# A state-space scan in chunks of 64 over pairs of batches, and a shorter seam before the experts

## The chip, the cores and the metric

The kernel runs on one core of a Trainium2 chip. Its time is the device time of one execution in microseconds (us). The core has the engines PE (matrix products; its weight loads are shown as PEld), DVE (vector), ACT (activation), POOL (general purpose) and SP, which here only issues DMA transfers; transfers that POOL issues go through indices. SBUF is the on-chip memory, PSUM the memory that PE writes, HBM the main memory. A `name<-a,b` in a row is the tile written and the tiles read.

## The reference

Two parts follow each other. The first is a scan over 4 batches, 8 heads and 768 places, with 32 columns of x and 16 of state per head:

```python
cum = cumsum(log(clip(a, 1e-6, 1)))          # within a chunk
L = exp(cum[i] - cum[j]) for i >= j, else 0
y = ((C @ B.T) * L) @ x + (C @ state) * exp(cum)
state = exp(cum[-1]) * state + (B * exp(cum[-1] - cum)).T @ x
```

The result does not depend on the size of the chunk but for rounding. Its rows, 3072 tokens of 256 numbers, go to the second part, which gives each token to one of 8 experts:

```python
logits = x @ w_gate;  e = argmax(logits);  gate = softmax(logits)[e]
out = gate * (relu(x @ w1[e]) @ w2[e])       # 256 -> 1024 -> 256
```

## The kernel before, in words

**Scan.** A tile is one batch and 128 places with all 8 heads; there are 24. For each, `decay` (L152) makes the lower triangle L of products of a: PE copies the tile's row of `az` to all 128 partitions (`abc`, L158, two fp32 matmuls of 512 columns, in which one row of the identity picks one of 24 rows), and DVE runs a product scan over them (L161, two of 512). `scores` (L181) is C times B for four heads at a time, 64 rows of the array each (`g`, L187), with C written four times under a mask by POOL (`masks`, `ctm`, L148), so that each head sees its own 16 rows. `weigh` (L191) multiplies g by L on DVE. `state` (L199) adds the tile's own part A (L205) to the carried state on DVE (L209 to L213); A is 128 by 256, and a mask `smask` keeps the blocks of each head. `y` (L217) adds the carried part (L223, through `ctd`, made on POOL from a second scan `dec` on DVE) and the part of the tile (L228: 8 matmuls, each on 32 columns of the array, with all 128 rows). `rows` (L236) turns the result to one token per partition and makes the 8 logits in the same matmuls (L245); ACT copies it out of PSUM.

**Routing.** Groups of 6 tiles are routed: `choose` (L253) takes the expert, and POOL counts on tile by tile (`cnt`, L272); `rank` (L279) makes each token's place by two matmuls; `place` (L292) sends each tile's 128 rows to the expert's list `x_hbm` in HBM by an indirect DMA of POOL.

**Experts.** `m_load` (L316) reads an expert's list back (448 places), `m_xT` (L336) transposes it, `m_h` (L354) and `m_y` (L369) are the two products, `m_half` (L377) the last 64 places of two experts together, and `put` (L360) scales and scatters rows to the output.

**Order.** It is written out by hand in the main loop (L428): every engine runs its own queue in the program's order. In one turn of the loop come decay and scores of tile n, the masks of tile n + 1, state and y of tile n - 1, weigh of tile n, rows of tile n - 2, and at times choose, rank and two places. All of the experts' weights (16 MB, L139) are loaded during the scan, three transfers for every three tiles. After the last tile the places of the last six tiles follow (L458), and then everything of `over` (L301, a check on overflow) and of the experts 0 and 1's lists before the first `m_h`.

Of the kernel before, what the change touches and what calls it, by code (L numbers as in the profile page):

```python
# [9 lines left out]
FP32 = mybir.dt.float32  # L10
# [20 lines left out]
NR = N + 128  # L31


@with_exitstack
def ssd_then_moe(ctx, tc, x, a, B, BT, CT, w_gate, w1, w2, out):
# [32 lines left out]

    oh_all = route.tile([128, NT, E], BF16, name="oh_all")
    cnt = route.tile([128, NT + 1, E], BF16, name="cnt")  # L70
# [4 lines left out]
    def scan_consts():  # L75
        make_identity(nc, ident)
        nc.vector.tensor_copy(turn[:, 0:128], ident)
        nc.vector.tensor_copy(turn[:, 128 + 2 * E:], ident)
        nc.vector.tensor_copy(ident4, bc(ident[:, None, :], [128, 4, 128]))
        nc.gpsimd.memset(hsel, 1.0)  # L80
        nc.gpsimd.affine_select(out=hsel, in_=hsel, pattern=[[-NS, NH]], base=0, channel_multiplier=1,
                                compare_op=ALU.is_ge, fill=0.0)
        nc.gpsimd.affine_select(out=hsel, in_=hsel, pattern=[[NS, NH]], base=NS - 1, channel_multiplier=-1,
                                compare_op=ALU.is_ge, fill=0.0)
        nc.vector.tensor_tensor(vmask, hsel[:, 0:4], hsel[:, 4:8], op=ALU.add)  # L85
        nc.vector.tensor_copy(smask, bc(hsel[:, :, None], [128, NH, D]))

    def route_consts():
        nc.gpsimd.memset(Tmat, 1.0)
# [5 lines left out]
        nc.vector.tensor_scalar(out=rev_e, in0=iota_i, scalar1=-1.0, scalar2=float(E), op0=ALU.mult, op1=ALU.add)  # L95
        nc.vector.tensor_scalar(out=base_e, in0=iota_i, scalar1=float(NR), scalar2=None, op0=ALU.mult)
        nc.gpsimd.iota(tok_i, pattern=[[128, NT]], base=0, channel_multiplier=1)
        nc.vector.memset(cnt[:, 0, :], 0.0)
# [4 lines left out]
        nc.gpsimd.tensor_copy(zrows[:, :, DM + 1].bitcast(I32), none_i)  # L103
        for e in range(E):
            nc.sync.dma_start(out=x_hbm[e * NR:e * NR + CAP, :].rearrange("(p c) w -> p c w", c=CAP // 64),
                              in_=zrows)
# [5 lines left out]
    def clip(ap):  # L112
        nc.vector.tensor_scalar(out=ap, in0=ap, scalar1=1e-6, scalar2=1.0, op0=ALU.max, op1=ALU.min)

    def load_a():
        for b in range(NB):
            nc.sync.dma_start(out=az[b * NC:(b + 1) * NC], in_=a[b].rearrange("h (c i) -> c h i", i=128))
        clip(az)
        nc.vector.memset(az[:, :, 0:1], 0.0)  # L119

    def load(g):
        b, s0 = divmod(g * CG * 128, S)
        c0 = s0 // 128
        r = gr[g]
        T = CG * 128
        r["CT"] = ld.tile([128, T], FP32, name="ct")
        nc.sync.dma_start(out=r["CT"], in_=CT[b, :, s0:s0 + T])
        r["BT"] = ld.tile([128, T], FP32, name="bt")
        nc.sync.dma_start(out=r["BT"], in_=BT[b, :, s0:s0 + T])
        r["a"] = ld.tile([128, T], FP32, name="ar")  # L130
        nc.sync.dma_start(out=r["a"], in_=bc(a[b, :, None, s0:s0 + T], [NH, NS, T]))
        r["B"] = ld.tile([128, CG, NH * NS], FP32, name="bn")
        nc.sync.dma_start(out=r["B"], in_=B[b, :, c0:c0 + CG, :])
        r["x"] = ld.tile([128, CG, DM], FP32, name="xn")
        nc.sync.dma_start(out=r["x"], in_=x[b, :, c0:c0 + CG, :])
# [5 lines left out]
    def at(k, nm):  # L141
        c = k % CG
        t = gr[k // CG][nm]
        return t[:, c * 128:(c + 1) * 128] if len(t.shape) == 2 else t[:, c]

    def masks(k):
        m = wk.tile([128, 4, 128], FP32, name="ctm")
        nc.gpsimd.tensor_tensor(out=m, in0=bc(at(k, "CT")[:, None, :], [128, 4, 128]),  # L148
                                in1=bc(vmask[:, :, None], [128, 4, 128]), op=ALU.mult)
        st[k]["ctm"] = m  # L150

    def decay(k):  # L152
        s = st[k]
        s["L"] = wk.tile([128, NH, 128], FP32, name="L", bufs=3)
        s["bcast"] = []
        for t in range(2):
# [8 lines left out]
    def decay_in(k):  # L165
        s = st[k]
        if k % CG == 0:
            clip(gr[k // CG]["a"])
# [22 lines left out]
    def weigh(k):  # L191
        s = st[k]
        for t in range(2):
            d = s["L"][:, 4 * t:4 * t + 4, :]
            nc.vector.tensor_tensor(out=d, in0=s["g"][t], in1=d, op=ALU.mult)  # L195
# [327 lines left out]
```

## Time and profile before

| what | value |
|---|---|
| median of 3 runs | 388.58 us (387.5 to 389.88) |
| profiled execution | 386.13 us, span 384.4 us, mean granted clock of PE 0.945 |
| PE busy | 343.3 us (89%), PEld 206.1 us |
| DVE, POOL, ACT busy | 135.7, 108.7, 71.2 us |
| DMA | 40.41 MB, mean 105 GB/s |
| scan's first DVE scan of the second tile | at 12.99 us |
| last matmuls of the scan's last tile | start at 147.60 us |
| first `m_h` matmul | starts at 173.72 us |

The span runs from the first to the last instruction. A matmul's end is modelled, so a busy PE does not mean one at its peak; the start of the next group says more. An fp32 matmul of the program stands as two in the trace, with a weight load each. [...] The first stretch of the page shows a clock of 1.00, while matmuls there last twice as long as later ones; the durations are to be believed.

### The profile page before, as it was taken

Reading aid. Unit: us, or ns where it says so; the run is one execution under the profiler, and the core shown is the slowest. Engines: PE = TensorE matmul, PEld = TensorE weight load, DVE = VectorE, ACT = ScalarE, POOL = GpSimd, SP = SyncE. Lnnn points to the kernel's source line nnn. Section 1 sums busy time; section 2 is a strip of 40 time slices with the busy share of each in tenths; the row PEclk is TensorE's granted clock in tenths of the full one; section 3 lists DMA queues with packets and bytes.
Section 4 is the critical chain, followed back from the end, with each engine's and each line's share of the span. In section 5 each row is a group of like instructions: output and inputs, shape, how many; then the busy total and the mean of one; then the engine's idle time right before and its main releaser. Section 6 shows DMA issues by size and latency. Waiting matters only on the chain.

```text
span 384.4 us, 4487 instructions
## 1 busy us (share of the span) xinstructions
PE 343.3 (89%) x1625; PEld 206.1 (54%) x1625; DVE 135.7 (35%) x261; ACT 71.2 (19%) x193; POOL 108.7 (28%) x193
## 2 busy tenths in 40 slices
PE   4999999999899893039999999999999999999992
PEld 1354445545454452025558558576586675766881
DVE  5699888887888883111110010010010100000000
ACT  1011120111011212002230221312312213222110
POOL 5323344374348528600002202113011031120321
PEclk9999997899899988558999999999999999999997
DMA  6999999888301002161000201102002010000011
GB/s 188 281 208 341 373 373 386 338 298 294 135 29 52 5 0 83 69 167 40 0 0 30 67 0 43 38 14 77 14 14 69 3 37 0 13 28 0 29 35 32
DMA packets 15622, 40.41 MB, mean 105 GB/s; under 512 B 2597, under 2 KB 10471, under 8 KB 13544
## 3 DMA queue, kind: packets, MB, share of 16 engines
q1 hardware_dynamic: 13096, 33.72, 26.9%
q0 software_dynamic: 2496, 6.32, 4.6%
q8 instruction: 15, 0.25, 0.3%
q14 instruction: 15, 0.12, 0.1%
HBM read 30.02 MB, written 10.54 MB: 106 GB/s over the span
## 4 chain that ended last, share of the span: by engine, by line
issue 52%; PE 19%; POOL 17%; DVE 8%; DMA 1%; POOLq 1%; SPq 0%; DVEq 0%
POOL out_dram L363 7%; PE abc L158 6%; PE g L187 5%; POOL x_hbm L294 4%; DVE L L161 3%; DVE L L195 3%; PE A L205 2%; PE y L228 2%; POOL bs L178 2%; PE rows_ps L245 2%; POOL ctm L148 1%; POOL cnt L272 1%; PE y L223 1%; POOL ctd L173 1%; DMA x_hbm<-rows,pos 1%
## 5 line engine op out<-in xcount | busy, mean ns | idle before, releaser
L351 PE MATMUL h_ps<-xT,w 128*128 128x448 f32 x256 | 98.6, 544 | 0.0
L373 PE MATMUL y_ps<-w,hT 128*128 128x256 f32 x384 | 84.3, 380 | 0.0
L373 PEld LDWEIGHTS y_ps<-w,hT 128*128 128x128 f32 x384 | 72.7, 190 | 10.5 <-issue 1.1
L363 POOL DMA_INDIRECT out_dram<-yo,xs x24 | 23.6, 984 | 178.1 <-ACT yo L362 178.1
L351 PEld LDWEIGHTS h_ps<-xT,w 128*128 128x128 f32 x256 | 48.8, 192 | 46.2 <-issue 46.1
L161 DVE TENSOR_TENSOR_SCAN L<-abc,ident 128x512 f32<-128x512 f32 x48 | 56.1, 1206 | 2.0 <-PE abc L158 1.7
L158 PE MATMUL abc<-az,ident 24*128 24x512 f32 x96 | 51.3, 655 | 6.1 <-DVE az L119 5.1
L358 ACT ACTIVATE hT<-h_ps 128x448 f32<-128x448 f32 x64 | 34.8, 543 | 89.3 <-PE h_ps L351 89.3
L187 PE MATMUL g<-ctm,bt 64*128 64x512 f32 x96 | 33.0, 736 | 3.6 <-POOL ctm L148 3.6
L195 DVE TENSOR_TENSOR L<-g,L 128x512 f32<-128x512 f32 x48 | 30.9, 685 | 10.0 <-POOL bs L178 9.7
L345 DVE COPY xT<-xT_ps 128x256 f32<-128x256 f32 x24 | 9.6, 420 | 58.6 <-PE xT_ps L333 58.6
L173 POOL TENSOR_TENSOR ctd<-ct,dec 128x128 f32<-128x128 f32 x24 | 10.9, 454 | 67.8 <-DVE dec L170 59.6
L342 DVE COPY xT<-xT_ps 128x128 f32<-128x128 f32 x8 | 2.0, 286 | 79.1 <-PE xT_ps L333 79.1
L231 ACT COPY yT<-y 128x256 f32<-128x256 f32 x24 | 8.9, 372 | 112.8 <-PE y L228 112.8
L158 PEld LDWEIGHTS abc<-az,ident 24*128 24x128 f32 x96 | 16.8, 195 | 23.5 <-issue 10.6
L362 ACT ACTIVATE yo<-y_ps,xs 128x256 f32<-128x256 f32 x24 | 11.4, 473 | 78.2 <-PE y_ps L373 78.2
L294 POOL DMA_INDIRECT x_hbm<-rows,pos x24 | 23.7, 987 | 6.2 <-issue 4.2
L148 POOL TENSOR_TENSOR ctm<-ct,vmask 128x512 f32<-128x512 f32 x24 | 24.9, 1039 | 0.6 <-DVE vmask L85 0.6
L187 PEld LDWEIGHTS g<-ctm,bt 64*128 64x128 f32 x96 | 9.3, 205 | 23.7 <-issue 10.6
L245 PE MATMUL rows_ps<-turn,yT 128*128 128x136 f32 x96 | 18.1, 313 | 0.6 <-ACT lg L250 0.6
L228 PE MATMUL y<-L,xn 128*32 128x128 f32 x384 | 16.3, 288 | 0.4 <-DVE L L195 0.4
L205 PEld LDWEIGHTS A<-xn,bs 128*128 128x128 f32 x40 | 6.8, 212 | 18.1 <-issue 9.1
(79 smaller groups left out, 204.6 us busy)
## 6 DMA issues: line engine op xcount, KB each, us to landing
w<-in_w_dram SPq DMA_DIRECT2D x16, 1024.0 KB, 11.6
x_hbm<-zrows SPq DMA_DIRECT2D x8, 451.5 KB, 7.8
xs<-x_hbm SPq DMA_DIRECT2D x24, 129.0 KB, 2.2
xn<-in_x_dram SPq DMA_DIRECT2D x8, 384.0 KB, 5.7
ct<-in_CT_dram SPq DMA_DIRECT2D x8, 192.0 KB, 7.3
bt<-in_BT_dram SPq DMA_DIRECT2D x8, 192.0 KB, 2.5
ar<-in_a_dram SPq DMA_DIRECT2D x8, 192.0 KB
bn<-in_B_dram SPq DMA_DIRECT2D x8, 192.0 KB, 4.2
```

The costliest lines, as they stand in the source:

```text
L148: nc.gpsimd.tensor_tensor(out=m, in0=bc(at(k, "CT")[:, None, :], [128, 4, 128]), in1=bc(vmask[:, :, None], [128, 4, 128]), op=ALU.mult)
L158: nc.tensor.matmul(p, lhsT=bc(ident[0:NT, k:k + 1], [NT, 128]), rhs=az[:, 4 * t:4 * t + 4, :].rearrange("p h i -> p (h i)"), start=True, s ...
L161: nc.vector.tensor_tensor_scan(out=s["L"][:, 4 * t:4 * t + 4, :].rearrange("p h i -> p (h i)"), data0=p, data1=ident4.rearrange("p h i -> ...
L187: nc.tensor.matmul(g.rearrange("p h i -> p (h i)"), lhsT=at(k, "BT")[sl, :], rhs=s["ctm"][sl].rearrange("p h i -> p (h i)"), start=True, s ...
L195: nc.vector.tensor_tensor(out=d, in0=s["g"][t], in1=d, op=ALU.mult)
L228: nc.tensor.matmul(p[D * q:D * q + D, t], lhsT=at(k, "x")[:, D * h:D * h + D], rhs=s["L"][:, h], start=(not inter and t == 0), stop=True, ...
L245: nc.tensor.matmul(p[:, 128 * t:128 * t + 128 + E], lhsT=st[k]["yT"][:, t], rhs=turn[:, (128 + E) * t:(128 + E) * (t + 1)], start=(t == 0) ...
L294: s_ = nc.gpsimd.indirect_dma_start(out=x_hbm[:, :], out_offset=bass.IndirectOffsetOnAxis(ap=pos[:, k:k + 1], axis=0), in_=rt[k // RG]["ro ...
L351: nc.tensor.matmul(p[:, 0:n], lhsT=w[:, c:c + 128], rhs=xT[:, t], start=(t == 0), stop=(t == KT - 1))
L358: nc.scalar.activation(ex[e]["hT"][:, f], p, func=ACT.Relu)
L363: s_ = nc.gpsimd.indirect_dma_start(out=out[:, :], out_offset=bass.IndirectOffsetOnAxis(ap=xs[:, DM + 1:DM + 2].bitcast(I32), axis=0), in_ ...
L373: nc.tensor.matmul(p, lhsT=ex[e]["hT"][:, f, 128 * t:128 * t + 128], rhs=w_sb[e][1][:, f * DM:f * DM + DM], start=(f == 0), stop=(f == FT ...
```

## The change

- A tile is now 64 places of two batches (64 partitions each), with all 8 heads. The number of tiles stays 24. The triangle L of 8 heads is then 128 by 512, half of before.
- `az` (a per tile and head) is laid out by the host as 96 rows, three times the same; `split_az` cuts it into three bfloat16 parts that add up to it, and one bfloat16 matmul per tile (`a_rows`) with three ones per column adds them while it copies the row to 64 partitions per batch. It is issued a turn ahead.
- The matmuls of scores, own part, carried part and weighed part are cut into blocks of 32 or 64 rows and 32 or 64 columns of the array: 8, 16, 8 and 16 of them per tile (`scores`, `own`, `y`).
- Two masked copies of C in place of four, made by ACT for four tiles at a time; `dec` and `ctd` for four tiles at a time; clip and preparation of a on POOL.
- rows and logits are copied out of PSUM by one ACT instruction; the lists' rows are 266 numbers wide in place of 258.
- Routing in groups of 6, 6, 6, 4 and 2 tiles; rank right behind choose, by matmuls that sum the earlier tiles of a group themselves, in place of POOL's counts.
- Weights of experts 0 to 3 are loaded in the scan, those of 4 to 7 in the experts' stage, into memory that the scan has left. An expert's list is read by one DMA in place of three. `over` and the transposes of expert 1 stand within the first `m_h`, those of expert e + 1 in the middle of the `m_h` of e.

```diff
+RGS = [6, 6, 6, 4, 2]
...
+        eng.tensor_copy(z, f)
+        eng.tensor_tensor(out=f, in0=f, in1=z, op=ALU.subtract)
+        eng.tensor_copy(z[32:64], f[32:64])
+        eng.tensor_copy(z[64:96], f[64:96])
...
+        nc.tensor.matmul(t, lhsT=selx[:, 2 * c:2 * c + 2].rearrange("p c j -> p (c j)"), rhs=azp[p],
+                         start=True, stop=True)
...
+        nc.gpsimd.tensor_tensor(out=bs[n % 2][:, :, 0:4:3, :], in0=b, in1=bc(l, [128, 4, 2, NS]), op=ALU.mult)
+    def scores(n):
+        c = n % CG
+        g = ps.tile([128, 2, 512], FP32, name="g", bufs=1)
+        for s in range(2):
+            for t in range(2):
+                for v in range(2):
+                    r = slice(64 * t + 32 * v, 64 * t + 32 * v + 32)
+                    o = c * 128 + s * CH
+                    nc.tensor.matmul(g[64 * t:64 * t + 64, v, 128 * s:128 * s + 128],
+                                     lhsT=gr[n // CG]["BT"][r, o:o + CH],
+                                     rhs=gr[n // CG]["ctm"][r, c, s].rearrange("p u i -> p (u i)"),
+                                     start=(s == 0), stop=(s == 1), skip_group_check=True)
...
+        for s in range(2):
+            for u in range(2):
+                for t in range(2):
+                    for v in range(2):
+                        r = slice(64 * t, 64 * t + 64)
+                        o = (4 * s + 2 * v + u) * D
+                        nc.tensor.matmul(
+                            A[32 * (2 * t + v):32 * (2 * t + v) + 32, s, D * u:D * u + D],
+                            lhsT=bs[k % 2][r, 2 * s + v, 2 * u:2 * u + 2, :].rearrange("p u m -> p (u m)"),
+                            rhs=xk[r, o:o + D], start=(s == 0 and u == 0), stop=(s == 1 and u == 1),
+                            skip_group_check=True)
...
+            o = (k % CG) * 128 + CH - 1
+            for s in range(2):
+                nc.vector.scalar_tensor_tensor(out=new[:, s], in0=carry[k][:, s],
+                                               scalar=gr[k // CG]["dec"][:, o + s * CH:o + s * CH + 1],
+                                               in1=A[:, s], op0=ALU.mult, op1=ALU.add)
...
+            for s in range(2):
+                for t in range(2):
+                    for v in range(2):
+                        r = slice(64 * t + 32 * v, 64 * t + 32 * v + 32)
+                        o = (k % CG) * 128 + s * CH
+                        nc.tensor.matmul(p[64 * v:64 * v + 64, t, s * CH:s * CH + CH], lhsT=carry[k][r, s],
+                                         rhs=gr[k // CG]["ctd"][r, o:o + CH], start=(s == 0), stop=False,
+                                         skip_group_check=True)
+        for s in range(2):
             for q in range(4):
-                h = 4 * t + q
-                nc.tensor.matmul(p[D * q:D * q + D, t], lhsT=at(k, "x")[:, D * h:D * h + D], rhs=s["L"][:, h],
-                                 start=(not inter and t == 0), stop=True, skip_group_check=True)
-        s["yT"] = wk.tile([128, 2, 128], FP32, name="yT")
-        nc.scalar.copy(out=s["yT"], in_=p)
-    rt = [dict() for _ in range(NT // RG)]
+                for t in range(2):
+                    r = slice(64 * t, 64 * t + 64)
+                    o = (4 * s + q) * D
+                    nc.tensor.matmul(p[D * q:D * q + D, t, s * CH:s * CH + CH], lhsT=xk[r, o:o + D],
+                                     rhs=st[k]["M"][r, 4 * s + q], start=(not inter and s == 0), stop=True,
+                                     skip_group_check=True)
...
+        nc.scalar.copy(out=rt[g][:, k - R0[g], 0:DM + E], in_=p)
...
-        nc.tensor.matmul(p, lhsT=Tmat, rhs=oh_all[:, sl, :], start=True, stop=False)
-        nc.tensor.matmul(p, lhsT=ones_bf, rhs=cnt[:, sl, :], start=False, stop=True)
-        rb = sm.tile(sh, FP32, name="rb")
+        n = RGS[g]
+        sl = slice(R0[g], R0[g] + n)
+        sh = [128, n, E]
+        oh = oh_all[:, sl, :]
+        p = ps.tile(sh, FP32, name="rank", tag="rows", bufs=1)
+        nc.tensor.matmul(p, lhsT=ones_bf, rhs=bc(cnt[:, g:g + 1, :], sh), start=True, stop=False,
+                         skip_group_check=True)
+        for d in range(1, n):
+            nc.tensor.matmul(p[:, d:n], lhsT=ones_bf, rhs=oh[:, 0:n - d], start=False, stop=False,
+                             skip_group_check=True)
+        nc.tensor.matmul(p, lhsT=Tmat, rhs=oh, start=False, stop=True, skip_group_check=True)
...
+            if f == FT // 2:
+                between()
...
+                if 2 <= n < 6:
+                    for e in (2 * (n - 2), 2 * (n - 2) + 1):
+                        empty(e)
+                if n >= 6 and n % 2 == 0 and n < 22:
+                    load_w((n - 6) // 2)
                 decay(n)
+                if n == 0:
+                    decay_in(0)
+                    decay_C(0)
                 scores(n)
-                decay_in(n)
+                if n + 1 < NT:
+                    a_rows(n + 1)
                 scaled_B(n)
...
+                if g + 1 < NG:
+                    if c == 1:
+                        decay_a(g + 1)
+                    if c == 2:
+                        decay_in(g + 1)
+                        decay_C(g + 1)
+                        masks(g + 1)
+                if n == 5:
+                    split_az(nc.gpsimd, 1, azt)
+            j = k - 1
+            if 0 <= j < NT:
+                rows(j)
+                if j == R0[grp[j]] + RGS[grp[j]] - 1:
+                    exs[n + 1] = grp[j]
+            if n in exs:
+                q = exs[n]
+                e_ = choose(q)
+                rank(q)
+                gates(q, e_)
+                count(q)
+                todo += list(range(R0[q], R0[q] + RGS[q]))
+            elif todo:
+                for _ in range(2):
+                    if todo:
+                        place(todo.pop(0))
...
-        over(tb, pp)
...
-            m_xT(e, mo, pp)
+        m_xT(0, mo, pp)
         for e in range(E + 1):
+            def nxt():
+                if e + 1 < E:
+                    if e + 2 < E:
+                        m_load(e + 2, mo)
+                    m_xT(e + 1, mo, pp)
+                if e == 0:
+                    over(tb, pp)
+                if e < E - EW:
+                    load_w(2 * (e + EW))
+                    load_w(2 * (e + EW) + 1)
             if e < E:
-                m_h(e, mo, pp)
-            if e + 2 < E:
-                m_load(e + 2, mo)
-                m_xT(e + 2, mo, pp)
+                m_h(e, mo, pp, nxt)
```

On PE, one tile in the middle of the scan. Before (abc is the row of a, g the scores, A the own part, y first the carried and then the tile's part, rows_ps the turned rows):

```order
L158 MATMUL abc<-az,ident 128x512 x2
L187 MATMUL g<-ctm,bt 128x512 x2
L205 MATMUL A<-xn,bs 128x256
L223 MATMUL y<-ctd,S 128x128 x2
L228 MATMUL y<-L,xn 32x128 x8
L245 MATMUL rows_ps<-turn,yT 128x136 x2
```

and now, with the same names (M is the weighed triangle, S the carried state):

```order
L233 MATMUL g<-ctm,bt 64x128 x8
L208 LDWEIGHTS selx
L208 MATMUL abc<-azp_96,selx 128x512
L260 MATMUL A<-xn,bs_101 32x32 x16
L293 MATMUL y<-ctd,S 64x64 x8
L301 MATMUL y<-M,xn 32x64 x16
L315 MATMUL rows_ps<-turn,yT 128x136 x2
```

Seventeen matmuls of the program have become 51, of which 48 are small, and the row of a is now that of the next tile.

On POOL, the end of the scan, where the rows are sent to the lists. Before:

```order
L294 DMA x_hbm<-rows_922,pos_107 25600x258
L272 TENSOR_TENSOR cnt_106<-cnt_106,oh_all_105 128x8 x6
L277 COPY rows_1246<-tok_i_103 128x6
L293 MEMSET spare_109 1x1
L294 DMA x_hbm<-rows_1246,pos_107 25600x258
```

where the last pair stands six times, once for each tile of the last group, and now:

```order
L347 COPY rows3_110<-tok_i_90 128x4
L375 MEMSET spare_106 1x1
L376 DMA x_hbm<-rows3_110,pos_104 25600x266
L347 COPY rows4_111<-tok_i_90 128x2
L375 MEMSET spare_106 1x1
L376 DMA x_hbm<-rows3_110,pos_104 25600x266
L376 DMA x_hbm<-rows4_111,pos_104 25600x266
```

where the group of four goes out two and two around the copy for the last group, and the last group has two transfers; the counts are gone from this queue.

## Rows read from the trace of the kernel before

**Rows 1.** Windows: scan, seam, experts (length; busy time per engine with count; clock, DMA).
```profile
13.00:148.30 135.30, 129.75 (x788) 65.93 (x788) 114.09 (x195) 21.14 (x96) 63.25 (x120) 0.95 0.63 215
148.30:173.70 25.40, 4.34 (x18) 2.66 (x17) 5.64 (x25) 0.75 (x4) 10.74 (x25) 0.56 0.39 117
173.70:377.00 203.30, 201.17 (x812) 134.70 (x810) 8.70 (x25) 47.53 (x91) 26.57 (x27) 1.00 0.08 26
```

**Rows 2.** Chain that ended last, one tile undisturbed (start, us, what, instructions).
```profile
29.08 1.91 PE abc L158 x4
30.99 1.06 PE g L187 x4
32.05 0.63 PE A L205 x2
32.68 0.44 PE y L223 x4
33.12 0.57 PE y L228 x16
33.70 0.66 PE rows_ps L245 x4
34.36 1.91 PE abc L158 x4
```

**Rows 3.** PE's timeline, expert 7's first product (start, us, what, count).
```profile
340.44 12.19 PE L351 MATMUL h_ps<-xT,w 128*128 128x448 f32 x32
```

**Rows 4.** PE's timeline after its wait near 62 us.
```profile
62.65 2.46 PE L187 MATMUL g<-ctm,bt 64*128 64x512 f32 x4 [0.88 <-POOL ctm L148]
67.04 1.08 PE L228 MATMUL y<-L,xn 128*32 128x128 f32 x16
68.06 1.28 PE L245 MATMUL rows_ps<-turn,yT 128*128 128x136 f32 x4
```

**Rows 5.** Windows: the same stretch, the clock before the last two columns.
```profile
66.00:68.00 2.00, 2.00 (x21) 1.36 (x19) 1.67 (x3) 0.00 (x0) 1.44 (x3) 0.50 1.06 309
```

**Rows 6.** Timeline of PE and DVE at the scan's start.
```profile
5.13 3.75 PE L158 MATMUL abc<-az,ident 24*128 24x512 f32 x4 [5.13 <-DVE az L119]
12.99 1.21 DVE L161 TENSOR_TENSOR_SCAN L<-abc,ident 128x512 f32<-128x512 f32 x1
16.53 1.22 PE L205 MATMUL A<-xn,bs 128*128 128x256 f32 x2
17.68 0.85 PE L228 MATMUL y<-L,xn 128*32 128x128 f32 x16
```

**Rows 7.** Groups of instructions (busy us, mean ns of one, idle before and its cause).
```profile
L161 DVE TENSOR_TENSOR_SCAN L<-abc,ident 128x512 f32<-128x512 f32 x48 | 56.1, 1206 | 2.0 <-PE abc L158 1.7
L195 DVE TENSOR_TENSOR L<-g,L 128x512 f32<-128x512 f32 x48 | 30.9, 685 | 10.0 <-POOL bs L178 9.7
L148 POOL TENSOR_TENSOR ctm<-ct,vmask 128x512 f32<-128x512 f32 x24 | 24.9, 1039 | 0.6 <-DVE vmask L85 0.6
L294 POOL DMA_INDIRECT x_hbm<-rows,pos x24 | 23.7, 987 | 6.2 <-issue 4.2
```

**Rows 8.** Timeline of all engines in the seam.
```profile
147.60 0.73 PE L245 MATMUL rows_ps<-turn,yT 128*128 128x136 f32 x4 [0.59 <-ACT lg L250]
148.91 0.20 DVE L258 TENSOR_REDUCE mx<-lg 128x6 f32<-128x48 f32 x1 [3.04 <-ACT lg L250]
153.72 0.21 DVE L286 TENSOR_TENSOR rb<-rank,base_e 128x48 f32<-128x48 f32 x1 [2.97 <-PE rank L284]
155.42 1.00 POOL L294 DMA_INDIRECT x_hbm<-rows,pos  x1 [1.56 <-DVE fl L309]
161.82 0.97 POOL L294 DMA_INDIRECT x_hbm<-rows,pos  x1 [0.22 <-issue]
164.85 1.28 SPq L321 DMA_DIRECT2D xs<-x_hbm  x3
169.50 0.66 PE L333 MATMUL xT_ps<-ident,xh 128*128 128x128 f32 x2 [15.27 <-DMA xs<-x_hbm]
173.72 2.77 PE L351 MATMUL h_ps<-xT,w 128*128 128x448 f32 x5
```

More of the change, by code (lines that the diff above doesn't have):

```diff
@@ L109, in ssd_then_moe, with clip @@
     gr = [dict() for _ in range(NG)]
     st = [dict() for _ in range(NT)]
[L112 to L119, printed above, removed]
+    def clip(eng, ap):
+        eng.tensor_scalar(out=ap, in0=ap, scalar1=1e-6, scalar2=1.0, op0=ALU.max, op1=ALU.min)
@@ L139, in load_w @@
         nc.sync.dma_start(out=w_sb[e][u], in_=(w1, w2)[u][e])
[L141 to L156, printed above, removed]
-            p = ps.tile([128, 512], FP32, name="abc", bufs=2)
-            nc.tensor.matmul(p, lhsT=bc(ident[0:NT, k:k + 1], [NT, 128]),
-                             rhs=az[:, 4 * t:4 * t + 4, :].rearrange("p h i -> p (h i)"), start=True, stop=True)
-            nc.vector.tensor_tensor_scan(
-                out=s["L"][:, 4 * t:4 * t + 4, :].rearrange("p h i -> p (h i)"), data0=p,
-                data1=ident4.rearrange("p h i -> p (h i)"), initial=0.0, op0=ALU.mult, op1=ALU.add)
@@ L165, in decay_in @@
[L165 to L168, printed above, removed]
-        s["dec"] = wk.tile([128, 128], FP32, name="dec", bufs=3)
-        nc.vector.tensor_tensor_scan(out=s["dec"], data0=at(k, "a"), data1=bc(zero1, [128, 128]), initial=1.0,
-                                     op0=ALU.mult, op1=ALU.add)
-        s["ctd"] = wk.tile([128, 128], FP32, name="ctd", bufs=3)
-        nc.gpsimd.tensor_tensor(out=s["ctd"], in0=at(k, "CT"), in1=s["dec"], op=ALU.mult)
@@ L191, in weigh, with masks, decay_a @@
[L191 to L195, printed above, removed]
-    carry = {}
+    def masks(g):
+        m = wk.tile([128, CG, 2, 2, CH], FP32, name="ctm")
+        for u in range(2):
+            nc.scalar.mul(m[:, :, :, u, :], gr[g]["CT"].rearrange("p (c s i) -> p c s i", c=CG, s=2), par[:, u:u + 1])
+        gr[g]["ctm"] = m
+    def decay_a(g):
+        t = gr[g]["a"]
+        clip(nc.gpsimd, t)
+        nc.gpsimd.tensor_copy(d1[g % 2][:, :, 0:1], t[:, :, 0:1])
+        nc.gpsimd.memset(t[:, :, 0:1], 0.0)
@@ new lines, in decay_in, with decay_C @@
+    def decay_in(g):
+        r = gr[g]
+        r["dec"] = wk.tile([128, CG * 128], FP32, name="dec")
+        nc.vector.tensor_tensor_scan(
+            out=r["dec"], data0=r["a"].rearrange("p h i -> p (h i)"),
+            data1=d1[g % 2].rearrange("p h i -> p (h i)"), initial=0.0, op0=ALU.mult, op1=ALU.add)
+    def decay_C(g):
+        r = gr[g]
+        r["ctd"] = wk.tile([128, CG * 128], FP32, name="ctd")
+        nc.gpsimd.tensor_tensor(out=r["ctd"], in0=r["CT"], in1=r["dec"], op=ALU.mult)
@@ new lines, in y @@
+        nc.scalar.copy(out=st[k]["yT"], in_=p[:, :, 0:128])
+    rt = [sm.tile([128, n, W], FP32, name=f"rows{i}") for i, n in enumerate(RGS)]
+    grp = [g for g, n in enumerate(RGS) for _ in range(n)]
+    def rows(k):
+        p = ps.tile([128, DM + E], FP32, name="rows_ps", tag="rows", bufs=1)
+        for t in range(KT):
+            nc.tensor.matmul(p[:, 128 * t:128 * t + HB], lhsT=st[k]["yT"][:, t], rhs=turn[:, HB * t:HB * t + HB],
+                             start=(t == 0), stop=(t == KT - 1), skip_group_check=True)
+        g = grp[k]
+        nc.scalar.copy(out=rt[g][:, k - R0[g], 0:DM + E], in_=p)
```

337 lines of the change are left out of this document (180 added, 157 removed).

## The prediction

> **What bounds the kernel now.** I read the windows by stage first. The scan takes from 12.99 us [rows 6] to 148.3 with PE busy in 129.75 of 135.3 us, DVE in 114.09 and POOL in 63.25; the seam takes 25.4 us with PE nearly idle; the experts take the rest with PE at full clock and never idle [rows 1]. So three questions: what sets a tile's time in the scan, what the seam consists of, and whether the experts are touched. The chain of waits answers the first: in an undisturbed tile it stays on PE through all six groups of matmuls, from 29.08 to 34.36, 5.28 us [rows 2]. The 23 tiles from 12.99 to 148.3 average 5.88, because the chain leaves PE in some of them: at 62.65 PE had stood for the masks that POOL makes [rows 4].
>
> **The price of a matmul.** Expert 7's 32 matmuls of 448 columns end 12.19 us after they start [rows 3], 0.38 us each and 0.84 ns per column, at full clock. So 512 columns cost 0.43 us, 128 cost 0.107. With it each group of [rows 2] splits into streaming and a surplus. The 16 y matmuls on 32-column blocks would take 1.71 us one by one; they took 0.57 (33.12 to 33.69), so four blocks run side by side, 0.43, and 0.14 is surplus. The g group, four passes of 512 on two row blocks, is 0.86 and 0.20. abc, four passes in a row, is 1.71 and 0.20. I take 0.16 per group, and 0.027 us for one small matmul with its weight load (0.43/16).
>
> **PE, tile by tile, at full clock.** Each fp32 matmul is two passes: four abc stand for the two issued [rows 2]. Streaming now: scores 16 passes of 128 columns over four row blocks, 0.43. Own part 32 passes of 32 columns and weighed part 32 of 64: streaming alone would be 0.1 and 0.2, but no row shows a pair under 0.027, so 0.86 each. Carried part 16 passes, likewise 0.43. Turned rows, unchanged, 0.45. The row of a: one bfloat16 pass of 512 in place of four fp32 ones; no row has one of that size. Above, it is the fp32 pass, 0.43; below, half of it; I take 0.30. Sum 3.33, and six surpluses 0.96: **4.3 us per tile** for 5.28.
>
> **The other engines in a tile.** DVE: one product scan and one multiplication of 512 in place of two each, 1.21 + 0.69; two state updates of 64 elements, at most 0.69 each by the multiplication of 512, nearer 0.3; a quarter of a 512 scan for dec, 0.30 [rows 7]: 2.8 of 4.3, hidden. POOL: the masks (1.04 a tile) go to ACT, which was busy 21 of 135 us [rows 1, 7]; left are bs (about half of a ctm), an average of one place with its memset (0.99 + 0.3), and per four tiles a clip and ctd of 512 at about 1.04 each: some 2.5 of 4.3. In turns with two places it is about 4.4, bs of the next tile waits behind them, but own needs it a turn later. If that cover goes, each such turn costs PE at most the 1.3 of a place. `split_az` for the second pair sits on POOL in turn 5, eight instructions, three of 512 elements on 96 partitions and four on 32, each at most ctm's 1.04, about 5.6 us, against some 5.3 that bs of tile 6 has to spare: even, and once.
>
> **DMA.** The scan moved 215 GB/s at a share of 0.63 [rows 1], 29 MB. Now 8 MB of weights fewer pass it, 21 MB in some 110 us, the same rate; the eight moved transfers land in a stage that used 0.08 of the DMA and come four experts ahead. On SP the loads of weights stand behind the lists' loads, never ahead of those of the same turn, so I price both at nothing; without that cover expert 4 would wait.
>
> **Added on the path of the scan.** Three times inside the scan choose, rank, gate and count now follow one another in one turn. PE reaches rank at the turn's end and waits for DVE's five small operations behind weigh, then DVE waits for PE; 14 operations of 0.2 us (as mx, [rows 8]) lie on DVE in that turn, 2.8 + 2.8 against 4.3. I take 1.7 us each, 5 in all (0 if the queues slide by, 10 if rank also holds up the next scores). The first tiles run at the lower clock, see below: 4.
>
> **Start and end of the scan.** The second tile's DVE scan begins at 12.99 [rows 6]; the new prologue has a longer chain for a (eight operations on 96 by 512 ahead of the first matmul) and shorter first tiles; I take 12.5, from 11 to 16. Then 22 x 4.3 = 94.4, the 5 and the 4: 116 for the start of the last tile. Behind it come its own 4.3, y 1.6, rows twice 0.6, rank 0.6: 123.7 (before: 148.33, [rows 8]).
>
> **The seam.** Before, 25.4 us from the last matmul's end to the first product at 173.72 [rows 8]. Now: copy 0.45; five operations of choose at a pitch of 0.24, 1.2; rank 0.7; from rb to the first place 1.7 as at 153.72 to 155.42; four places of the group before may still stand ahead, 1.3; two places in place of six, 2.3; landing until the list can be read 2.06 (162.79 to 164.85); list to first transpose 3.5 in place of 4.65, since that transpose waited behind five DMAs and now waits for one that is three times larger (2.6 to 4.65); eight transposes of the 14 that took 4.22 us, 2.4. Sum **15.6**, ending at 139.3 in place of 173.72: -34.4. The other six transposes now cost 1.5 within the first product. Nothing else of the experts changes.
>
> **Sum.** The profiled execution took 386.13, 2.45 under the median of 388.58. 386.13 - 34.4 + 1.5 = 353.2; on the median's footing **356 us**.
>
> **The clock, and the rivals.** [...] At the start abc took 3.75 for the later 1.91 [rows 2, 6]; PE then had work without a gap, all of it on 24 or 64 rows, and was still slow at 16.53, where A took 1.22; only during y at 17.68, 0.85, did it speed up [rows 6]. [...] My forecast has full level from the fourth or fifth tile on: PE never stands for POOL's masks any more. Chance 0.42.
>
> *Rival 1, the lower level through the whole scan*, as before's first 12 us ran while matmuls used part of the array. Streaming doubles, surpluses stay (1.02 - 0.86 = 0.16, [rows 4]), pairs stay at 0.027: scores 0.86, own 0.86, weighed 0.86, carried 0.43 to 0.86, row of a 0.43 to 0.86, rows 0.91, surplus 0.96, about 5.65. 12.5 + 124.3 + 3.6, last tile and tail 10.2, seam 15.6: 166.2, that is 6 less: **383** (375 to 389). Chance 0.24; a level that changes within the scan, 360 to 375, another 0.10.
>
> *Rival 2, slower: the lower level, and a pair of weight load and small matmul costs 0.053 there*, as the y group's did (0.86/16; only an upper bound, as its streaming explains it). Own and weighed 1.71 each, carried 0.86: 7.6 per tile, seam starting at 196: **428**. From rival 1 on, 80 pairs per tile decide: at 0.030 per pair the gain is gone. [...] Chance 0.13.
>
> *Rival 3, the change does not do what it says: row blocks that write one PSUM bank do not run side by side.* At full level scores become 1.71, weighed 1.71, carried 0.86: 6.85 per tile, **416**. [Rows 2] speak against it for two row blocks in different banks and four column blocks; nothing shows both at once. Chance 0.06. POOL's bursts on the path at 1.3 a turn with two places, some 370: 0.05.
>
> **The numbers.** Likeliest 356. Range 343 to 391: the low end has pairs at 0.020 and the first transpose at its lower bound; the high end takes in rival 1; about 0.2 lies outside, above all rivals 2 and 3. A change of 1% (3.9 us) is what can be told from none. Faster by more: 0.42 + 0.10 + 0.05 and half of rival 1, 0.70. Within 1%: rival 1's upper part, 0.09. Slower: 0.21.
>
> **What the profile after would show.** A period of 4.3 us between abc matmuls with PE leading the chain, and own and weighed groups of about 1.0 us each, would bear out the price per pair; groups of 1.9 with a clock of 0.50 would be rival 2, a clock of 0.50 with groups of 1.0 rival 1, long groups at 1.00 rival 3. The scan should end near 124 us, the first product start near 139, and from there to the end it should take as long as before within 2 us. DVE's busy time per tile above 4 us, or a chain through POOL's places, would make the forecast wrong in a way not listed.

## The result, and the profile after

The changed kernel takes **344.13 us** (median of 4, 343.1 to 347.92) beside 388.39 for the kernel before: a ratio of 0.8875, 95% interval 0.8802 to 0.8947. The prediction was 356 us, 343 to 391. Medians in this document are of all runs of a kernel and the ratios of its fast runs; two of dma_late's four runs were slow, and one each of own_twice, fp32_a, pool_relief, seam_undo, seam_groups, relief_even, relief_444 and broadcast_thrice. The profiled execution took 344.13, with a span of 342.4. Windows of its stages (length; busy time per engine with count; clock; DMA share and GB/s), against [rows 1]:

```profile
12.03:113.48 101.45, 84.56 (x2336) 59.72 (x2336) 66.59 (x147) 23.70 (x61) 58.69 (x101) 0.81 0.66 216
113.48:130.65 17.17, 2.58 (x12) 1.55 (x11) 4.26 (x23) 0.59 (x2) 6.35 (x12) 0.58 0.42 135
130.65:342.40 211.75, 203.16 (x817) 135.50 (x817) 10.30 (x34) 48.01 (x92) 27.56 (x28) 0.98 0.18 67
```

From the second tile's scan to the last matmul's end there are 101.45 us in place of 135.34, the seam is 17.17 in place of 25.4, the experts take 1.1 us longer and the start is 1.0 shorter: 42.0 off the span, 33.9 of them in the scan. PE is no longer always busy there: 84.56 of 101.45 us, three times the matmul passes, at a mean granted clock of 0.81.

PE's timeline through one tile at full clock (granted 1.00), against [rows 2], and the parts of one at the lower level (granted 0.50):

```profile
90.54 0.67 PE L233 MATMUL g<-ctm,bt 32*64 32x128 f32 x16
91.14 0.39 PE L208 MATMUL abc<-azp,selx 96*128 96x512 bf16 x1
91.46 0.46 PE L260 MATMUL A<-xn,bs 64*32 64x32 f32 x32
91.84 0.46 PE L293 MATMUL y<-ctd,S 32*64 32x64 f32 x16
92.23 0.46 PE L301 MATMUL y<-M,xn 64*32 64x64 f32 x32
92.61 0.73 PE L315 MATMUL rows_ps<-turn,yT 128*128 128x136 f32 x4
93.43 0.67 PE L233 MATMUL g<-ctm,bt 32*64 32x128 f32 x16
...
41.88 1.13 PE L233 MATMUL g<-ctm,bt 32*64 32x128 f32 x16
43.69 0.65 PE L260 MATMUL A<-xn,bs 64*32 64x32 f32 x32
44.27 0.70 PE L293 MATMUL y<-ctd,S 32*64 32x64 f32 x16
46.71 1.13 PE L233 MATMUL g<-ctm,bt 32*64 32x128 f32 x16
```

Starts are subtracted, since the ends overlap. The tile takes 2.89 us at full clock (90.54 to 93.43), where 4.3 was forecast; the 32 passes of the own part take 0.38, **0.012 us per pass with its weight load**. At the lower level the tile takes 4.83 and a pass 0.018. Were every tile 2.89, 24 of them would be 69 us; of the other 32, some 17 are time in which PE stands (101.45 - 84.56) and some 15 mostly the longer groups of the lower level. These are the largest of PE's waits (us in total, times, longest), and the rows of its timeline that end a stop:

```profile
PE A L260 <- POOL bs L223: 4.5, 2, 2.6
PE g L233 <- DVE M L242: 3.5, 4, 1.3
PE y L301 <- issue: 3.4, 3, 1.5
PE A L260 <- issue: 2.1, 1, 2.1
```

```profile
29.57 0.25 PE L260 MATMUL A<-xn,bs 64*32 64x32 f32 x3 [2.08 <-issue]
35.46 0.66 PE L301 MATMUL y<-M,xn 64*32 64x64 f32 x25 [0.92 <-issue]
58.25 0.67 PE L301 MATMUL y<-M,xn 64*32 64x64 f32 x29 [0.98 <-issue]
68.77 0.59 PE L260 MATMUL A<-xn,bs 64*32 64x32 f32 x26 [1.88 <-POOL bs L223]
75.05 0.30 PE L301 MATMUL y<-M,xn 64*32 64x64 f32 x4 [1.46 <-issue]
```

Four of these stops (2.08, 0.92, 0.98, 1.46 us) cut a group in two (x29, then x3), and the profile names nothing that PE waited for there (`issue`). The windows between them (first count: matmul passes):

```profile
29.57:35.46 5.89, 4.97 (x127) 3.35 (x127) 4.04 (x8) 0.75 (x2) 2.97 (x5) 0.62 0.88 213
35.46:58.25 22.79, 19.73 (x508) 13.88 (x507) 15.13 (x36) 5.02 (x13) 12.54 (x19) 0.72 0.97 351
58.25:75.05 16.80, 13.46 (x382) 9.50 (x382) 10.09 (x16) 4.03 (x10) 12.43 (x20) 0.80 0.71 245
```

127, 508 and 382 are 1, 4 and 3 times 127 (to one): the stops lie on a grid of instructions. Counted from the first matmul, they stand before passes 347, 474, 982 and 1363, each 93 more than a multiple of 127. The profile also has a DMA queue that it names instruction (packets, MB, share), before, now, and in own_twice below:

```profile
q8 instruction: 15, 0.25, 0.3%
q8 instruction: 27, 0.44, 0.5%
q8 instruction: 32, 0.52, 0.6%
```

PE had 1625 matmul passes before, has 3182 now and 3886 in own_twice, each with a weight load: 12 packets more for 3114 more instructions, 5 more for 1408, so one packet of some 16 KB per 260 to 280. 127 matmuls and as many weight loads are 254 instructions, close to that. So I read the stops as PE waiting for its own instructions: that is an inference, no row names what ended them and no run shows it apart. The lower level follows stops, too: 31.0 to 48.0, 58.4 to 61.7, 68.6 to 71.9 and 75.4 to 89.0 us have a granted clock of 0.50, each beginning within 1.5 us of the end of a stop above. Not every stop was followed so: PE also stood 1.28 us before 55.28 and 1.29 us before 104.70, both for DVE's M, and the clock stayed at 1.00.

On POOL, two groups of the scan (busy us, mean ns, idle before), against [rows 7]; a place costs what it did, the clip has no row there:

```profile
L139 POOL TENSOR_SCALAR ar<-ar 128x512 f32<-128x512 f32 x5 | 9.6, 1921 | 0.4
L376 POOL DMA_INDIRECT x_hbm<-rows,pos x18 | 18.7, 1041 | 5.0 <-issue 1.6 <-ACT yT L305 1.4 <-DMA w<-in_w_dram 0.9
```

And the seam on all engines, against [rows 8]:

```profile
112.75 0.73 PE L315 MATMUL rows_ps<-turn,yT 128*128 128x136 f32 x4 [0.28 <-DVE rb L363]
114.73 0.98 POOL L376 DMA_INDIRECT x_hbm<-rows,pos  x1 [1.86 <-DVE eq L334]
115.97 0.17 DVE L367 CAST pos<-rf 128x2 int32<-128x2 f32 x1
121.16 0.96 POOL L376 DMA_INDIRECT x_hbm<-rows,pos  x1 [0.22 <-issue]
124.48 0.40 SPq L400 DMA_DIRECT2D xs<-x_hbm  x1
127.92 1.92 PE L412 MATMUL xT_ps<-ident,xs 128*128 128x128 f32 x6 [12.62 <-issue]
130.65 1.11 PE L431 MATMUL h_ps<-xT,w 128*128 128x448 f32 x1 [0.39 <-DVE xT L425]
```

Six places, some 1.3 us apart, stand between the scan's end and the first list.

### The profile page after: what moved, and what is told of

Read it like the earlier page. It is cut to its first block, busy times and chain, and to the rows that moved or that the text cites. A ratio compares the mean times of both kernels' runs of the same rounds, so it can differ in the third digit from the quotient of the medians.

```text
span 342.4 us, 7382 instructions
## 1 busy us (share of the span) xinstructions
PE 292.6 (85%) x3182; PEld 197.7 (58%) x3182; DVE 89.1 (26%) x217; ACT 76.9 (22%) x162; POOL 99.5 (29%) x164
## 4 chain that ended last, share of the span: by engine, by line
issue 54%; POOL 8%; POOLq 1%
POOL out_dram L445 8%; POOLq L445 0%; POOL x_hbm L376 0%; POOLq L594 0%
## 5 line engine op out<-in xcount | busy, mean ns | idle before, releaser
L216 DVE TENSOR_TENSOR_SCAN L<-abc,ident 128x512 f32<-128x512 f32 x24 | 29.0, 1210 | 0.6 <-POOL spare L375 0.6
L233 PE MATMUL g<-ctm,bt 32*64 32x128 f32 x384 | 22.0, 360 | 6.2 <-DVE M L242 3.5
L233 PEld LDWEIGHTS g<-ctm,bt 32*64 32x64 f32 x384 | 14.3, 175 | 16.1 <-ACT ctm L183 7.6
L412 PE MATMUL xT_ps<-ident,xs 128*128 128x128 f32 x48 | 9.0, 300 | 14.9 <-issue 12.6
L208 PE MATMUL abc<-azp,selx 96*128 96x512 bf16 x24 | 12.0, 499 | 7.5 <-DVE azp L157 7.5
L315 PEld LDWEIGHTS rows_ps<-turn,yT 128*128 128x128 f32 x96 | 16.5, 239 | 3.1 <-issue 1.2
L223 POOL TENSOR_TENSOR bs<-bn,L 128x128 f32<-128x128 f32 x24 | 9.8, 414 | 27.9 <-DVE L L216 21.2
L260 PE MATMUL A<-xn,bs 64*32 64x32 f32 x704 | 12.0, 214 | 6.7 <-POOL bs L223 4.5
L260 PEld LDWEIGHTS A<-xn,bs 64*32 64x32 f32 x704 | 9.3, 125 | 14.1 <-POOL bs L223 7.3
L412 PEld LDWEIGHTS xT_ps<-ident,xs 128*128 128x128 f32 x48 | 5.9, 150 | 19.9 <-issue 15.6
L301 PE MATMUL y<-M,xn 64*32 64x64 f32 x768 | 14.2, 255 | 3.4 <-issue 3.4
```

Source lines behind the costliest of these rows:

```text
L208: nc.tensor.matmul(t, lhsT=selx[:, 2 * c:2 * c + 2].rearrange("p c j -> p (c j)"), rhs=azp[p], start=True, stop=True)
L216: nc.vector.tensor_tensor_scan(out=s["L"].rearrange("p h i -> p (h i)"), data0=s["abc"], data1=ident8.rearrange("p h i -> p (h i)"), initi ...
L233: nc.tensor.matmul(g[64 * t:64 * t + 64, v, 128 * s:128 * s + 128], lhsT=gr[n // CG]["BT"][r, o:o + CH], rhs=gr[n // CG]["ctm"][r, c, s].r ...
L260: nc.tensor.matmul(A[32 * (2 * t + v):32 * (2 * t + v) + 32, s, D * u:D * u + D], lhsT=bs[k % 2][r, 2 * s + v, 2 * u:2 * u + 2, :].rearran ...
L301: nc.tensor.matmul(p[D * q:D * q + D, t, s * CH:s * CH + CH], lhsT=xk[r, o:o + D], rhs=st[k]["M"][r, 4 * s + q], start=(not inter and s == ...
L315: nc.tensor.matmul(p[:, 128 * t:128 * t + HB], lhsT=st[k]["yT"][:, t], rhs=turn[:, HB * t:HB * t + HB], start=(t == 0), stop=(t == KT - 1) ...
```

## The experiments

Three sets of four, each against runs of the kernel before on the same chip; each set had another chip. The changed kernel itself ran again only in the third, so in the first two a difference of some 3 us from 344.13 can be the chip's.

**own_twice**: the own part issued twice.
```diff
-        for s in range(2):
+        for s in (0, 1, 0, 1):
```


> The changed kernel with the own-part matmuls of every tile issued twice over (32 more passes with their weight loads per tile, 22 tiles; the second pass writes the same values). If one pass with its weight load costs the 0.012 us at full clock and 0.018 at the lower one that its trace shows and PE is the path: 13 x 0.39 + 9 x 0.58, less some 1.5 us in tiles where PE waits for something else: +9, 353 us (349 to 357). If a pass costs the 0.027 us of the prediction: +19, 363. If PE is not the path in most tiles: +0 to 3, 344 to 347.


360.85 us, ratio 0.9242 (0.9158 to 0.9327): +17. A tile's 64 passes in the timeline at full clock, a stop with a window around it, and two lines of PE's waits:
```profile
61.32 0.76 PE L260 MATMUL A<-xn,bs 64*32 64x32 f32 x64
62.00 0.46 PE L293 MATMUL y<-ctd,S 32*64 32x64 f32 x16
57.48 0.44 PE L260 MATMUL A<-xn,bs 64*32 64x32 f32 x27 [0.36 <-issue]
```
```profile
57.00:58.00 1.00, 0.64 (x47) 0.50 (x40) 0.04 (x1) 0.00 (x0) 0.00 (x0) 1.00 0.00 0
```
```profile
PE A L260 <- issue: 7.3, 7, 3.3
PE y L293 <- issue: 6.3, 4, 3.6
```
64 passes take 0.68 us, 0.011 each; other tiles take up to 1.02, at either level. PE's busy time grows by 9.8 us (302.4 from 292.6): the +9 of the small price. The rest is stops on the grid, 15.2 us (7.3, 6.3 and 1.6 ahead of weighed parts) for 5.4, with 704 matmul passes more. PE is the path. Short stops came here with nothing on the DMA queues, too: 0.36 us at 57.48 and 0.40 at 111.86, at 0 GB/s.

**fp32_a**: the row of a by one fp32 matmul, no splitting.
```diff
-        z = azp[p]
-        eng.tensor_copy(z, f)
-        ... (the seven splitting instructions)
+        azp[p] = f      # 24 rows, fp32; sel and selx fp32 too
```


> The changed kernel with the row of a broadcast by one fp32 matmul (24 rows, two passes of 512 columns) instead of a bfloat16 one on three parts (96 rows, one pass); the splitting instructions fall away. Two fp32 passes cost 0.95 us at full clock by the trace of before (1.91 for four) against 0.32: with PE as the path +0.63 in some 14 tiles and +1.3 in some 10 at the lower clock, less about 2.5 us of splitting at the start: +19, 363 us (355 to 370). If DVE or POOL paces the tiles: +0 to 8, 344 to 352. If the splitting on POOL and DVE is what held the start: below 344.


366.28 us, ratio 0.9362 (0.927 to 0.9455): +22, the expected cost of a PE path. Its abc at full clock:
```profile
123.66 1.12 PE L201 MATMUL abc<-az,selx 24*128 24x512 f32 x2
124.71 0.46 PE L253 MATMUL A<-xn,bs 64*32 64x32 f32 x32
```
1.05 us in place of 0.32. The bfloat16 split is worth half of what the change gained. Stops on the grid fell to 2.0 us; that PE, slower per tile, leaves the supply more time would fit, but no run shows it apart.

**dma_late**: weights in turns 14 to 21, empty rows one per turn.
```diff
-                if 2 <= n < 6: two empty() per turn;  n >= 6, even: load_w((n - 6) // 2)
+                if 1 <= n < 9: empty(n - 1);          14 <= n < 22: load_w(n - 14)
```


> The changed kernel, except that the eight weight loads of the scan are issued one per turn in turns 14 to 21 (before: every other turn from 6) and the eight writes of empty rows one per turn in turns 1 to 8 (before: two per turn in turns 2 to 5). Same bytes, same instructions on PE. Theory: PE's stops in the middle of a group (2.08 us at 27.5, 0.92 at 34.5, 0.98 at 57.3, 1.46 at 73.6) are PE waiting for its own instructions, since between neighbours lie 127, 508 and 381 matmuls (1, 4 and 3 times 127), and they show only where the DMA queues are full; the stretches at clock 0.50 that follow them go with them. Then the stops at 57.3 and 73.6 and the low stretches at 58.8 and 75.7 vanish: 2.4 us of stops, and 13.3 us at the lower clock shrink by about 5: 336 us (329 to 339 if the stops at the start go too). Rival A: the clock falls for a reason of its own: only stops go, 341 to 343. Rival B: the stops are places in the program and not transfers: 344, same places. Rival C: weights land too late for the experts: above 346, with PE standing between experts.


350.88 us, ratio 0.9032 (0.8922 to 0.9142): no gain (the two lower runs took 345.81 and 348.3). The grid's points at 29 and 58 us (passes 347 and 982) passed without a stop. The stop before pass 1363 stayed and grew from 1.46 to 2.62, and new ones came before pass 601 (1.84 us at 39.19) and, where the weights now went, before pass 1617; by PE's timeline and a window around the last (GB/s last):
```profile
75.61 0.30 PE L301 MATMUL y<-M,xn 64*32 64x64 f32 x4 [2.62 <-issue]
89.63 0.32 PE L260 MATMUL A<-xn,bs 64*32 64x32 f32 x12 [2.17 <-issue]
```
```profile
86.00:90.00 4.00, 1.83 (x59) 1.15 (x61) 1.00 (x2) 0.65 (x2) 3.60 (x6) 1.00 1.01 404
```
So where a stop can be is set by the program, and whether and how long it is by something else: rival B falls. In the first and third set every stop of 0.9 us or more stands on the grid with a DMA share of 0.73 or more (from 1 us before it to its end). The short ones of own_twice show that a stop needs no full queues, and from 35.46 to 58.25 us the changed kernel passed three points of the grid (601, 728 and 855) at a share of 0.97 without one. That full queues lengthen the stops fits all of this; moving the bytes only moved the long ones.

**pool_relief**: clips on DVE, routing constants behind the first bs.
```diff
-        clip(nc.gpsimd, t)
+        clip(nc.gpsimd if g == 0 else nc.vector, t)
-        route_consts()                  # ahead of the loop
+                if n == 0: route_consts()   # behind scaled_B(0)
```


> The changed kernel, except that the clip of a (128 x 512, 1.92 us on POOL) runs on DVE for all groups but the first, and the routing constants are made behind the first bs instead of ahead of it. Theory: PE's waits for POOL's bs (2.6 us at 14 us, 1.9 at 66.9) come from POOL's queue, so both go, and with the second the low clock at 69.3: about 340 us (337 to 342). Rival: DVE, which now carries five clips more, paces the tiles: 344 to 347, with PE waiting for M in more tiles. Rival: what waits at 14 us is hidden behind transfers of the start: 342 to 344.


344.2 us, ratio 0.8835 (0.8746 to 0.8923). That is the changed kernel's time, within the two intervals. PE's waits for bs fell from 4.5 to 0.8 us, but its stops on the grid came to 9.2 for 5.4: the wait was taken away and not its time.

**w_later**, **seam_undo**, **seam_groups**, **rank_later** were the second set.
```diff
 w_later:     -  load_w in turns 6 to 20   +  expert 0's in turns 20, 21; the others behind m_load(0), m_load(1)
 seam_undo:   -RGS = [6, 6, 6, 4, 2]       +RGS = [6, 6, 6, 6]; m_xT(1) behind m_xT(0)
 seam_groups: -RGS = [6, 6, 6, 4, 2]       +RGS = [6, 6, 5, 4, 3]
 rank_later:  -choose, rank in one turn    +rank, gates, count in the next
```


> The changed kernel, with the weights of expert 0 loaded in turns 20 and 21 and those of experts 1 to 3 behind the first two experts' lists, so that no weight crosses the scan's first 19 turns; the bytes are the same. Theory: PE's stops in the middle of a group are fetches of PE's instructions that stand behind data on the DMA queues. The run with later weights moved them: none near 57 us, where the queues now were light, and longer ones (2.62, 2.17 us) from 75 on, where the weights now were. So here no stop between 40 and 95 us; those at 27 and 34 us stay, with the loads and the empty rows. If the lower clock follows stops, the stretch at 76 to 89 goes too and the scan ends 5 to 8 us earlier, 337 to 340 us. Rival: the clock falls again for another reason: scan 1 to 3 us shorter, 341 to 344. Rival: weights of expert 1 late: PE stands between experts, 345 or more.

> The changed kernel with two parts of the seam undone: the tiles in four groups of six, and expert 1's transposes ahead of expert 0's products. If these parts shortened the seam as forecast: the last rank is one of six tiles, six places of 1.27 us follow it where the last of six ended 6.2 us after pos, so +1.5 to 2; six more transposes ahead of the first product, 1.7 to 2.4 us; the first product 3 to 4 us later against the end of the scan (20 to 21.5 us in place of 17.2), and 1 us back within the experts: 346 to 347.5. Rival: choose with its rank saved once in the scan's tail gives 1 to 2 us back: 344 to 346. Rival: the seam was shortened by nothing but the single load of a list: seam 17 to 18 us, 344.

> The changed kernel with groups of 6, 6, 5, 4 and 3 tiles in place of 6, 6, 6, 4 and 2. Theory: the seam is set by POOL's queue of places, six of which (1.27 us apart) lay behind the scan's end because the fourth group's rank came only with the last tile. Now that group is ranked in turn 23 and placed in turns 24 and 25, and three places are left: last place 6.2 - 2.4 = 3.8 us after pos, seam 14.5 to 15.5 us in place of 17.2; the fourth choose now lies beside a full tile, +1: 342.5 to 343. Rival: the places land one after the other whatever their issue, seam 17: 344 to 345.

> The changed kernel with rank, gates and count one turn behind choose. Theory of the forecast: each of three turns stalls PE for rank's inputs and the next M some 1.7 us (its trace: 0.67 at the rank at 50.6 and 1.28 at the g of 55.28, in sum about 2 per turn). If these are waits of queues, they go: -4 to -5, about 340. If DVE's 14 operations themselves fill DVE (2.8 us beside 2.8 of a tile of 2.9), the wait only moves to the next turn: -0 to -1.5, 343 to 344.


362.87, 365.66, 360.23 and 365.23 us, ratios 0.9359, 0.9396, 0.9266 and 0.9403, where the kernel before took 386.54. In two of them this is no effect of the edit: seam_undo runs the changed kernel's own program up to turn 19 and seam_groups up to turn 18, and both are 10 us behind it by then (g of turn 19 at 104.05 for 93.43, of turn 18 at 100.44 for 90.54). The edits of w_later and rank_later act from turns 6 and 8, so there it isn't shown. Only stages are compared. The seam of seam_undo:
```profile
131.48 1.27 PE L315 MATMUL rows_ps<-turn,yT 128*128 128x136 f32 x4 [0.47 <-ACT rows L318]
154.31 2.45 PE L431 MATMUL h_ps<-xT,w 128*128 128x448 f32 x3
```
21.6 us from the last matmul's end in place of 17.2, and 210.5 from there to the span's end in place of 211.75: the two parts give 4.4 and take back 1.3, a little over the 3 to 4 and 1 expected. seam_groups kept 17.2: seven places lay at and behind the scan's end, since its fourth rank came at 128.48, 2.9 us before that end, and the first of these places at 131.04, so its theory fell. w_later, which expected no stop between 40 and 95 us, has 2.93 us at 43.05 and 2.26 at 80.89, the second with its two weights on the queues (281 GB/s): that theory fell, too. rank_later's gain, if any, can't be read at this set's spread; its seam is 18.9.

**after_again**: the changed kernel.


> The changed kernel itself, as a control: in the second set of runs four edits that should each move it by 1 to 7 us all came out at 360 to 366 us, against 342 to 351 for two edits of the first set. If that set's chip runs this program slower (its traces show PE stopping 8 to 15 times for 0.2 to 0.4 us within groups from 69 us on, which the first traces don't), the control gives 344 here or some 360 according to the chip, beside 386 to 390 for the kernel before. If those edits were slow of themselves, the control gives 342 to 348 wherever it runs.


347.07 us, ratio 0.8962 (0.8914 to 0.901). The control doesn't show the second set's slowness. The changed kernel was not run on that set's chip, so whether the chip or, in w_later and rank_later, the edit made it stays open.

**relief_even**: pool_relief, and weights as halves, one per turn from 5 to 20.
```diff
+                if 5 <= n < 21:  # half hf of weight (n - 5) // 2
+                    nc.sync.dma_start(out=w_sb[e][u][:, hf:hf + 1024], in_=(w1, w2)[u][e][:, hf:hf + 1024])
```


> The changed kernel with five of six clips on DVE, the routing constants behind the first bs, and the weights loaded as halves of 512 KB, one per turn from 5 to 20, instead of 1 MB every other turn. Theory: with POOL's queue out of the way (PE's waits for bs fell from 4.5 to 0.8 us in the run that moved the clips) what is left are stops for instructions, and bursts of data lengthen them; even loads shorten those at 34 to 76 us by 1 to 3 us: 3 to 6 us under the control. Rival: the stops have their places and lengths whatever the data's pace: 0 to 1 us under the control.


**341.75 us**, ratio 0.8808 (0.8769 to 0.8847), clear of the control's interval: 1.5% faster, the lowest median of all versions, though not told from pool_relief's by the intervals. But its reason isn't the one given: stops on the grid are 12.4 us beside 7.3. What fell is the wait for bs (4.3 to nothing above 0.5) and the time at the lower clock (mean of the span 0.934 beside 0.909). Which of the two edits does it isn't told apart; the clips and constants alone, on another chip, gave nothing (pool_relief).

**relief_444**: pool_relief with groups of 6, 6, 4, 4, 4.
```diff
-RGS = [6, 6, 6, 4, 2]
+RGS = [6, 6, 4, 4, 4]
```


> The changed kernel with the clips and constants moved as before, and groups of 6, 6, 4, 4 and 4 tiles, so that no place of the fourth group is left when the last is ranked and four places follow the last rank in place of six: last place 5.1 us after pos instead of 6.2, seam 16 us instead of 17.2; one more choose within the scan, +1 to 1.5: 0 to 1 us under the control. If places of the fourth group are left all the same (as with 6, 6, 5, 4, 3, where seven stood behind the scan's end): seam 17 or more, 1 to 2 over the control.


350.69 us, ratio 0.8995 (0.8928 to 0.9062): not better than the control. Its first product starts 17.5 us behind the last matmul's end (119.1 to 136.64), as the second case had it; the rest of the 3.6 us over the control isn't explained.

**broadcast_thrice**: two more broadcasts per tile, written over.
```diff
+        for _ in range(2 if n else 0):
+            nc.tensor.matmul(t, lhsT=selx[:, 0:2]..., rhs=azp[p], start=True, stop=True)
```


> The changed kernel with the bfloat16 broadcast of a issued three times per tile from the second on (the first two are written over): two more passes of 512 columns on 96 rows, 0.26 to 0.32 us each at full clock by its trace, 0.5 at the lower one. If the lower clock follows PE's stops, as the order of events suggests (each stretch at 0.50 begins 1 to 2 us behind a stop of 0.9 to 2.6), it stays as long as before and the passes add 0.55 x 14 + 1.0 x 9: +17 us over the control. If it is the sparse use of the array that holds the clock down, the stretches (34 us) shrink and give back up to 13: +0 to 8. If dense work lowers it, more than +20.


350.88 us, ratio 0.9077 (0.9017 to 0.9138): +4 over the control, not +17: the second case. The same stretches of the control and of this kernel:
```profile
24.00:60.00 36.00, 31.70 (x769) 22.12 (x763) 19.29 (x46) 6.64 (x17) 16.95 (x26) 0.68 0.87 284
60.00:90.00 30.00, 24.70 (x714) 17.58 (x710) 21.53 (x45) 7.92 (x20) 19.61 (x34) 0.81 0.63 233
90.00:113.00 23.00, 19.82 (x613) 14.34 (x612) 16.53 (x39) 5.56 (x15) 13.86 (x27) 0.85 0.13 45
```
```profile
24.00:60.00 36.00, 29.20 (x778) 18.53 (x777) 20.27 (x45) 7.69 (x20) 17.43 (x25) 0.91 0.89 281
60.00:90.00 30.00, 25.19 (x739) 16.54 (x742) 22.09 (x45) 7.91 (x20) 20.14 (x34) 0.94 0.65 244
90.00:113.00 23.00, 20.13 (x670) 13.85 (x670) 17.32 (x44) 6.15 (x16) 13.42 (x27) 1.00 0.12 40
```
With 46 passes more, 12 to 15 us of work at full clock, the clock stands at 0.91 to 1.00 in place of 0.68 to 0.85, and in the profiled runs the scan's last matmul starts at 114.9 in place of 115.8. The profiled run is the fastest of its four, so by the medians the added work paid for most of itself and not for all. One profile of each is a thin base (in the third stretch the first profile of the changed kernel has 1.00, too), but the mean clock of whole runs agrees: 0.912 to 0.950 in these four, 0.893 to 0.924 in the control's six. Stops as long (1.47 and 3.59 us) are still there, so stops alone don't set the clock.

## Why the prediction was right, and where it was not

The direction and the order of the gains held: PE bounds the scan (own_twice, fp32_a), blocks run side by side (rival 3: 16 passes of 128 columns in 0.60 us), the seam and the experts came within 2 us. The time itself lies 12 us under the 356, and only 1 us inside the range's low end. By its steps:

- **The price per pass was the mis-sized term.** "No row shows a pair under 0.027" was a bound, and I took it as the value, because it was the nearest row. It is 0.012 at full clock, 0.018 at the lower: own and weighed part 0.38 in place of 1.02 each, carried 0.39 for 0.59. The tile is 2.89, not 4.3; that alone would have put the scan's end some 31 us earlier (22 x 1.4). Rival 2's 0.053 falls: the measured 0.018 decides.
- **Full clock from the fifth tile on failed.** The level changed within the scan, the case given 0.10; its time was far under the 360 to 375 of that case because the pass was cheap. The forecast's reason, that PE never stands for POOL's masks any more, came true (ACT makes them now; before, PE had stood 0.88 us for them ahead of 62.65 [rows 4], and from 66 to 68 us the clock stood at 0.50 [rows 5]), but PE stood for other things: 4.5 us for POOL's bs, and for a reason not listed, 5.4 us of stops on the grid, which came with the many small passes; before, no group of the scan was cut by one.
- **POOL was priced too low.** The clip took 1.92, not 1.04, ctd 1.27, and `split_az` 8.0 for 5.6, which cost PE next to nothing. PE's two waits for bs, 4.5 us, had other causes on POOL's queue: at the start the routing constants and a ctd stood ahead of bs (10.01 to 15.95 us), and at 66.9 two places (65.74 to 68.29), which cost 1.9 where at most 1.3 was allowed for.
- Choose and rank: 1.7 forecast; the turn at 50 us stood 0.47 and 0.20 at the rank and 1.28 at the next g, 1.95.
- Scan's end 113.5 for 123.7, so some 21 of the 31 us were lost to clock, stops and waits; two errors of opposite sign made the sum look better than its terms. That the time fell inside the range is owed to this, and is luck.
- Seam 17.2 for 15.6: to the last place's end 8.6 for 7.65, landing 2.4 for 2.06, list to transposes 3.44 for 3.5, transposes 2.7 for 2.4. The experts' +1.1 stands for +1.5. On the profiled footing 353.2 - 10.2 + 1.6 - 0.4 is 344.2.

What stays open: what decides that a point of the grid stops PE, and for how long (0.2 to 3.9 us), what takes the clock down, and why the second set ran slower, with stops off the grid as well (1.20 us at 69.8 in w_later, 532 passes behind the one at 43.05).

## What to carry to other kernels

A bound read from the nearest row is a bound: when a change multiplies small operations, carry the end of the range that no row excludes as a case of its own. Splitting matmuls into blocks was cheap here in PE time, 0.012 us per pass at full clock, but it took PE's passes from 1625 to 3182, and 5.4 us of stops came with them, the long ones where the kernel's own data filled the DMA queues (a share of 0.73 or more, first and third set). A wait that is removed need not give its time back: in pool_relief 3.7 us of waits for bs went, the stops grew by 3.8 and the time stayed at 344.2. Look at the clock of the stretch first.

## What the hardware showed that was not expected

- PE stops in the middle of a group, 0.2 to 3.6 us, at fixed points 127 matmul passes apart (the first and third set, to within 5 passes). Those of 0.9 us and more stood beside 201 to 428 GB/s on the DMA queues, shorter ones also beside none. In the experts none shows (PE's longest wait from 130.65 us on is 0.4, for DVE's xT); at their start, with 408 GB/s from 130 to 140 us, PE makes only 26 passes, so at most one point of the grid lies there.
- At the start the profile grants 1.00 and the g group at 22.79 still takes 1.13 us, as it does at 0.50; a tile later (26.13) it takes 0.67.
- With 46 matmul passes of 512 columns added over the scan, the granted clock from 24 to 60 us was 0.91 in place of 0.68.
- A clip of 128 x 512 on POOL takes 1.92 us, a product of two tensors of that size there 1.04 [rows 7].
